# Two weight loads and two casts change places in GpSimd's opening queue

## Chip, core and metric

The kernel runs on one core of a Trainium2 chip. The metric is the device time of one execution in microseconds (us), the median of several runs. A core has five engines that work side by side and meet only at semaphores: TensorE (PE, matrix products; PEld is its loading of weights), VectorE (DVE), ScalarE (ACT), GpSimd (POOL) and SyncE (SP, which here only issues transfers). Transfers (DMAs) are issued by SP, ACT or GpSimd, each into a queue of its own, and are carried out by 16 DMA engines that all the queues share.

## What is computed

Attention over 8 batches, 8 heads, 576 positions and head size 64, followed by a gated feed-forward block over the 4608 token rows. Heads 0 to 3 see a window of the last 32 positions ("plain"), heads 4 to 7 every fourth position of the last 128 ("dilated"):

```python
mask_plain = (rel >= 0) & (rel < window)
mask_dil = (rel >= 0) & (rel < window * dilation) & (rel % dilation == 0)
attn = softmax(where(mask, scale * q @ k.T, -1e9))     # per batch and head
x = (attn @ v).transpose(0, 2, 1, 3).reshape(4608, 512)
out = (gelu(x @ w_gate) * (x @ w_val)) @ w_out         # 512 -> 1536 -> 512
```

Inputs and output are 32-bit floats in memory; the kernel computes in 16-bit floats.

## The kernel before

**Tiling.** Attention is cut into 32 units, four for each batch: a unit is a pair of heads. Units 0 and 1 of a batch are plain, 2 and 3 dilated. For a unit, PE makes scores (S), ACT takes the exponential (P), PE makes the denominators (D) and numerators (N), and DVE multiplies the numerator by the reciprocal (X), which writes 576 columns of one of the four `xT` tiles. The feed-forward part is cut into 8 chunks of 512 tokens. A chunk has a gate phase (line 597: 12 column blocks of 128, each with four products for the gate and four for the value, one per `xT` tile) and an output phase (line 604). The attention of batch c+1 is woven into the output phase of chunk c. The order of every engine is written out by hand, as strings of words in `gate_words` and `out_words`: "N1@00" is the numerators of unit 1, "X1" its multiplication, a bare number that many feed-forward products.

**The opening.** Batch 0 has to be computed before there is anything to weave it into. Its order on PE ends with

```python
"... N0@40 X0 D3@00 N2@60 X2 A3 N3@20 1 N1@00 X1 X3 G V 15 g0 u0 g1 u1 8 g2 u2 8 ..."
```

so N0, D3, N2, N3, one feed-forward product, N1, then 15 more products (with the one, column blocks 0 and 1), then block after block of 8. PE takes them strictly in this order.

**Block-diagonal v.** For units 0 and 1 of batch 0 the numerators use v in a block-diagonal form, the tile `vdiag`, 128 columns for each of 9 blocks of 64 positions. `load_v(0, 0, True)` (line 665) issues four loads on SP's queue, one for each half (64 partitions) of each unit, into the 32-bit tile `stage` (line 235). `cast_diag(g)` (lines 250 to 255) copies unit g out of `stage` into `vdiag` on GpSimd, in two casts of 64 partitions x 576 columns; each waits for its own load. N0 waits for the casts of unit 0, N1 for those of unit 1.

**Weights.** `w_gate` and `w_val` are loaded in four pieces of columns, `WC` (line 77): piece 0 holds column blocks 0 and 1, piece 1 blocks 2 and 3, piece 2 blocks 4 to 7, piece 3 blocks 8 to 11. `load_w(i)` (line 148) issues two loads, `wg` then `wv`, on GpSimd's queue; they turn 32-bit into 16-bit on the way. GpSimd has 8 semaphores for its loads and takes them in turn, so the issue of a load waits until the load eight places before it has landed.

**GpSimd's queue** is, in this order: masks; four loads of q and k of the dilated heads (line 176, into tails of `xT`); six loads of v (lines 295 and 303); `load_w(0, 1)`; the four casts of `vdiag`; `load_w(2)`; then, from `second()` (line 686), `load_w(3)`, two loads of q and k of batch 1 (line 690), two more (line 176), three of `w_out` (`wo`, line 156), six of v, and the masks of line 312 on.

**What hangs on it later.** `second()` also issues `load_v(1, 1, True)` on SP: the four loads of v for batch 1, which `gated` holds back until the first load of `w_out` has landed. GpSimd casts them at line 248, and N4, the first numerators of batch 1 (line 432), waits for that cast.

Of the kernel before, what the change touches and what calls it, by code (L numbers as in the profile page):

```python
# [21 lines left out]
def kernel(  # L22
# [125 lines left out]
    def load_w(*parts):  # L148

        for i in parts:  # L150
            for t, w in ((wg_t, moe_w_gate), (wv_t, moe_w_val)):
                src = w[:, WC[i][0] : WC[i][1]].rearrange("(kc p) n -> p kc n", p=P)
                nc.gpsimd.dma_start(out=t[i], in_=src)
# [43 lines left out]
    def st_of(i):  # L197
        return stage[:, 1280 * i : 1280 * i + 1280]
# [51 lines left out]
    def cast_diag(g):  # L250

        st = st_of(0)[:, 0:1152].rearrange("p (e d) -> p e d", d=D)
        at = slice(NB2 * g, NB2 * g + NB2)
        for x in range(2):
            nc.gpsimd.tensor_copy(diag[half_of(x), at, half_of(x)], st[half_of(x), at])  # L255

    def half_of(x, swap=0):
        y = x ^ (1 if swap else 0)
        return slice(64 * y, 64 * y + 64)
# [138 lines left out]
    def bias_first(n, bank):  # L398

        base = base_of(n, bank)  # L400
        tiles["bias", n] = True

        def part(c0, step, k, w, src=None, st=False):
            rhs = at2(bias, BQ if src else 0, [[0, k], [1, w]])
            o = at2(psf, base + c0, [[step, k], [1, w]])
            nc.tensor.matmul(o, ident, rhs, start=st, stop=False, skip_group_check=True)

        if is_plain(n):
            part(0, BQ, 5, BQ, st=True)
            part(5 * BQ, BQ, 3, BQ, st=True)  # L410
            part(8 * BQ, BK, 1, BK)
        else:
            part(0, 176, 3, BQ, st=True)
            part(BQ, 176, 2, 80)
            part(2 * 176 + BQ, 176, 2, 80, st=True)
            part(3 * 176, 176, 1, BQ)
            part(LD - BK, BK, 1, BK, src=True)
# [260 lines left out]
    biases()  # L678
    zero()
    bias_first(0, 4)  # L680
    load_w(0, 1)
    for g in range(2):
        cast_diag(g)
    load_w(2)

    def second():
# [170 lines left out]
```

## Time and profile before

| | us |
|---|---|
| median of 3 runs (328.08 to 329.41) | 328.7 |
| the profiled execution | 329.31 |
| its span, first to last instruction | 327.6 |
| PE busy in the span | 320.5 |
| GpSimd busy in the span | 78.6 |
| DMA engines, first third of the span | nearly always busy |

The span is what the profiler saw of one execution; the 1.71 us between it and that execution's own time lie around it. PE is busy 98% of the span, so a stall of PE shows nearly one for one in the time, and there is little else to gain or lose. All waits of PE fall into the first 53 us: after that no wait of PE is recorded. The first line of the slices of the profile shows how busy the DMA engines are over the span (40 slices of 8.19 us, in tenths):

```profile
DMA  8999996998897898989889657972000100020002
```

A row of the timeline below gives start, duration, engine, line, operation, output and input, the number of instructions merged, and in brackets the idle time ahead of it with what ended it. A row of the chain of waits gives start, duration and what the chain went through. Times in both count from the start of the span.

### The profile page before, as it was taken

How to read it: one execution, taken by the hardware profiler on the slowest of the kernel's cores; microseconds unless marked ns; L12 is line 12 of the kernel's file. 1: busy time of each engine (PE TensorE's matmuls, PEld its weight loads, DVE VectorE, ACT ScalarE, POOL GpSimd, SP SyncE). 2: the span in 40 equal slices, each digit the busy share in tenths (PEclk: the TensorE clock that was granted, in tenths of full speed). 3: DMA queues.
4: the chain of work that ended last, by engine and by line, in shares of the span. 5: the costliest groups of instructions: out<-in, count | busy, mean ns of one | idle time of the engine just before them, and what ended most of it. 6: DMA issues, size and time to landing. Idle time of an engine off the chain costs nothing.

```text
span 327.6 us, 7705 instructions
## 1 busy us (share of the span) xinstructions
PE 320.5 (98%) x3191; PEld 155.8 (48%) x3191; DVE 138.8 (42%) x208; ACT 169.5 (52%) x258; POOL 78.6 (24%) x126
## 2 busy tenths in 40 slices
PE   7899999999999999999999999999999999999995
PEld 4754544444544454445444454445444544444443
DVE  6763545434443444333633344334443354204410
ACT  2663566535863576347734783368436853234321
POOL 8783453402331340233224113311000000000000
PEclk9999999999999999999999999999999999999999
DMA  8999996998897898989889657972000100020002
GB/s 187 184 198 206 202 194 143 258 192 192 189 257 166 163 197 168 251 212 200 206 202 249 150 170 182 226 180 75 30 0 33 68 35 0 0 105 25 0 34 96
DMA packets 106659, 47.70 MB, mean 146 GB/s; under 512 B 83584, under 2 KB 102144, under 8 KB 106624
## 3 DMA queue, kind: packets, MB, share of 16 engines
q1 hardware_dynamic: 96352, 39.47, 52.4%
q0 software_dynamic: 9712, 7.08, 14.2%
q10 hardware_dynamic: 560, 0.66, 0.7%
q8 instruction: 25, 0.41, 0.5%
q14 instruction: 10, 0.08, 0.1%
HBM read 37.75 MB, written 9.44 MB: 144 GB/s over the span
## 4 chain that ended last, share of the span: by engine, by line
PE 83%; DMA 14%; SPq 1%; POOL 1%; issue 0%; DVE 0%; POOLq 0%
PE ps L597 51%; PE ps L604 26%; DMA stage<-in_v_dram 5%; PE ps L432 5%; DMA wo<-in_moe_w_out_dram 5%; DMA wg<-in_moe_w_gate_dram 2%; DMA u_all<-in_q_dram 2%; SPq L235 1%; PE ps L628 1%; POOL v L248 0%; POOL vdiag L255 0%; SPq L662 0%; DVE osb L637 0%; POOLq L248 0%
## 5 line engine op out<-in xcount | busy, mean ns | idle before, releaser
L759 DVE SCALAR_TENSOR_TENSOR u_all<-g,ps 128x512 f16<-128x512 f16 x108 | 74.2, 688 | 105.8 <-PE ps L597 92.2
L754 ACT ACTIVATE g<-ps 128x512 f16<-128x512 f32 x108 | 64.4, 597 | 104.4 <-PE ps L597 104.4
L597 PE MATMUL ps<-xT,wg 128*128 128x512 f16 x432 | 114.7, 379 | 0.2
L597 PE MATMUL ps<-xT,wv 128*128 128x512 f16 x432 | 114.0, 379 | 0.5 <-DMA wv<-in_moe_w_val_dram 0.5
L604 PE MATMUL ps<-wo,u_all 128*128 128x512 f16 x420 | 97.0, 380 | 0.0
L597 PEld LDWEIGHTS <-wv 128*128 128x128 f16 x432 | 42.1, 98 | 51.9 <-DMA wv<-in_moe_w_val_dram 1.2
L597 PEld LDWEIGHTS <-wg 128*128 128x128 f16 x432 | 42.1, 98 | 50.8 <-DMA wg<-in_moe_w_gate_dram 0.2
L604 PEld LDWEIGHTS <-u_all 128*128 128x128 f16 x420 | 38.7, 98 | 44.5 <-issue 0.3
L588 DVE TENSOR_TENSOR xT<-ps,rb 128x576 f16<-128x576 f32 x32 | 28.8, 938 | 27.1 <-PE ps L432 23.9
L462 ACT ACTIVATE P<-ps 128x832 f16<-128x832 f32 (+1 forms) x32 | 25.3, 834 | 14.4 <-PE ps L432 14.4
L248 POOL CAST v<-stage 128x1152 f16<-128x1152 f32 x13 | 15.0, 1154 | 67.5 <-DMA stage<-in_v_dram 67.5
L615 ACT ACTIVATE osb<-ps 128x512 f32<-128x512 f32 x31 | 18.5, 598 | 21.3 <-PE ps L604 20.9
L211 POOL CAST s<-stage 128x640 f16<-128x640 f32 x24 | 17.0, 735 | 39.0 <-DMA stage<-in_q_dram 23.7
L559 ACT ACTIVATE lg<-ps 128x576 f32<-128x576 f32 x30 | 18.2, 650 | 4.2 <-issue 2.2
L565 ACT ACTIVATE rb<-lg 128x576 f32<-128x576 f32 x30 | 19.0, 688 | 0.1
L223 POOL CAST s<-stage 128x512 f16<-128x512 f32 x24 | 14.4, 628 | 10.3 <-DMA stage<-in_q_dram 8.5
L467 DVE TENSOR_TENSOR P<-P,two_p 128x832 f16<-128x832 f16 x14 | 9.3, 670 | 13.4 <-ACT P L462 13.3
L467 DVE TENSOR_TENSOR P<-P,two_d 128x768 f16<-128x768 f16 x14 | 8.2, 592 | 13.2 <-ACT P L462 12.4
L779 ACT ACT_TABLE_LOAD x9 | 11.5, 1283 | 0.2
L432 PEld LDWEIGHTS <-q 64*64 64x64 f16 x576 | 7.7, 107 | 6.7 <-issue 5.5
L432 PEld LDWEIGHTS <-v 64*64 64x64 f16 x600 | 7.4, 107 | 5.9 <-issue 4.2
L432 PE MATMUL ps<-q 64*64 64x96 f16 (+2 forms) x576 | 9.9, 203 | 0.3 <-DVE q L334 0.3
(66 smaller groups left out, 123.0 us busy)
## 6 DMA issues: line engine op xcount, KB each, us to landing
out_dram<-osb SPq DMA_DIRECT2D x35, 256.0 KB, 3.2
stage<-in_v_dram SPq DMA_DIRECT2D x32, 144.0 KB, 3.5
stage<-in_q_dram SPq DMA_DIRECT2D x24, 128.0 KB, 3.5
stage<-in_k_dram SPq DMA_DIRECT2D x24, 128.0 KB, 2.9
stage<-in_q_dram SPq DMA_DIRECT2D x6, 512.0 KB, 4.8
stage<-in_k_dram SPq DMA_DIRECT2D x6, 512.0 KB, 5.6
stage<-in_v_dram SPq DMA_DIRECT2D x24, 128.0 KB, 3.0
wo<-in_moe_w_out_dram POOLq DMA_DIRECT2D x3, 512.0 KB, 15.9
```

The costliest lines, as they stand in the source:

```text
L211: nc.gpsimd.tensor_copy(s16[:, 1280 * t + 640 * g : 1280 * t + 640 * g + 640].rearrange("p (k c) -> p k c", k=5), st_of(i).rearrange("p (k ...
L432: nc.tensor.matmul(o[cols], lhs[rows], rhs[rows], start=st, stop=end, skip_group_check=True)
L462: nc.scalar.activation(pt[:, 0 : src.shape[1]], src, AF.Exp, bias=0.0, scale=scale)
L467: nc.vector.tensor_tensor(pt, pt, mask, ALU.mult)
L559: nc.scalar.activation(lg, psf[:, c0 : c0 + S], AF.Ln)
L565: nc.scalar.activation(rb, tiles.pop(("lg", n)), AF.Exp, scale=-1.0)
L588: nc.vector.tensor_tensor(dst, num, rb, ALU.mult)
L597: nc.tensor.matmul(ps[:, bank, :], w[:, kc, ns], xT[kc][:, tok], start=first, stop=end)
L604: nc.tensor.matmul(ps[:, bank, :], u_all[:, fc, tb * P : (tb + 1) * P], wo_t[fc // 4][:, fc % 4, :], start=(fc == 0), stop=(fc == NNB - 1),)
L615: nc.scalar.activation(osb, ps[:, bank, :], AF.Copy, bias=0.0, scale=1.0 / USCALE)
L754: nc.scalar.activation(g, ps[:, gate_banks(c, args[0])[0], :], AF.Gelu)
L759: nc.vector.scalar_tensor_tensor(u_all[:, nb, :], tiles.pop(("g", nb)), USCALE, val, ALU.mult, ALU.mult)
```

## The change

`load_w(0, 1)` is split: the casts of unit 0 go between weight piece 0 and piece 1, and those of unit 1 behind piece 1. Nothing else changes; the other engines keep their order, and the functions are as printed above.

```diff
     zero()
     bias_first(0, 4)
-    load_w(0, 1)
-    for g in range(2):
-        cast_diag(g)
+    load_w(0)
+    cast_diag(0)
+    load_w(1)
+    cast_diag(1)
     load_w(2)
```

In GpSimd's queue this gives: `wg` and `wv` of piece 0, two casts (unit 0), `wg` and `wv` of piece 1, two casts (unit 1), `wg` and `wv` of piece 2. The number of instructions is the same.

## The prediction

> **What bounds the kernel now.** I read the share of each engine first:
>
> ```profile
> PE 320.5 (98%) x3191; PEld 155.8 (48%) x3191; DVE 138.8 (42%) x208; ACT 169.5 (52%) x258; POOL 78.6 (24%) x126
> ```
>
> PE is the bound; a change on GpSimd counts only where it makes PE wait or stop waiting. So next the waits of PE (total, times, longest), up to 40 us and then from 27 to 60 us:
>
> ```profile
> PE ps L597 <- DMA wv<-in_moe_w_val_dram: 0.5, 1, 0.5
> PE ps L421 <- POOL vdiag L255: 0.4, 1, 0.4
> ...
> PE ps L432 <- POOL v L248: 0.3, 1, 0.3
> ```
>
> The same view from 56 us to the end is empty: whatever PE has lost by N4 (the third line) is lost for good, and nothing later takes it up. What holds N4 stands in the chain of waits of the first 60 us:
>
> ```profile
> 17.62 6.88 DMA wg<-in_moe_w_gate_dram
> ...
> 24.79 15.08 DMA wo<-in_moe_w_out_dram
> ...
> 41.90 9.43 DMA stage<-in_v_dram
> ...
> 51.48 1.16 POOL v L248
> ...
> 52.67 0.58 PE ps L432 x40
> ```
>
> From 17.62 to 52.67 us the chain runs through transfers, not through PE. N4 starts when the v of batch 1 has landed and is cast, and that v stands behind all the weights. The third place to look is GpSimd's timeline, where the change is made:
>
> ```profile
> 10.94 0.77 POOL L153 DMA_DIRECT2D wg<-in_moe_w_gate_dram  x1 [0.75 <-DMA xT<-in_q_dram]
> 11.70 0.76 POOL L153 DMA_DIRECT2D wv<-in_moe_w_val_dram  x1
> 12.96 0.74 POOL L153 DMA_DIRECT2D wg<-in_moe_w_gate_dram  x1 [0.51 <-DMA v<-in_v_dram]
> 13.69 0.75 POOL L153 DMA_DIRECT2D wv<-in_moe_w_val_dram  x1
> 14.42 0.68 POOL L255 CAST vdiag<-stage 64x576 f16<-64x576 f32 x1
> 15.43 1.38 POOL L255 CAST vdiag<-stage 64x576 f16<-64x576 f32 x2 [0.32 <-DMA stage<-in_v_dram]
> 17.01 0.67 POOL L255 CAST vdiag<-stage 64x576 f16<-64x576 f32 x1 [0.19 <-DMA stage<-in_v_dram]
> 17.62 0.74 POOL L153 DMA_DIRECT2D wg<-in_moe_w_gate_dram  x1
> ```
>
> The second cast of unit 0 starts at 15.43 because its v lands then, not because GpSimd comes late. Last, the DMA view from the start to 17 and to 18 us: q0 is GpSimd's queue, with packets, MB and share.
>
> ```profile
> q0 software_dynamic: 2655, 1.37, 60.5%
> ...
> q0 software_dynamic: 3028, 1.55, 64.8%
> ```
>
> The loads ahead of the weights are four of 144 KB, four of 64 and two of 16, 0.885 MB; with the two 256 KB pieces of `load_w(0)` 1.409 MB. That amount is passed between 17 and 18 us, at 17.2: there the engines begin piece 1. The trace's landing marks, sixteen for each load, agree: `wv` of piece 0 marks at 17.2 to 17.7 on 14 DMA engines, at 19.0 and 19.3 on two that lag; piece 1's `wg` at 18.5 to 19.0, the laggards at 19.8 and 20.6. Spacing is 1.3 us per 256 KB, 2.5 per 512 KB, with no gap.
>
> **What the Trainium skill says.** "DMA: Bandwidth & Descriptors", section "Queues, rings and completion order": each DMA engine works off its own ring of a queue in order and alternates between queues. The evenly spaced marks agree. The same page, "Why a DMA increments its semaphore by 16 and not by 1": a load has landed only when all its engines have marked, so the slowest decides; PE's wait for `wg` of piece 0 indeed ended at 18.00, with the last mark (17.95), not with the first fifteen (16.0 to 16.4). Its "Latency and other measured facts" gives about 1 us from a GpSimd load to its first byte. The trace does not agree: the first such load is issued at 3.16 and the 6.0 to 6.2 us window is the first that shows a packet of q0, 3.0 us after the issue begins. And "TensorE: Matmul & The Clock Gate", Part 1, says PE slows after about 3.4 us of idleness; the waits below are shorter, and the granted clock is 1.00 in every 2 us window of the first 56 us.
>
> **The change part by part.** GpSimd: both loads of piece 0 as before, to 12.46. The first cast of unit 0 waits for its v (last mark 14.21), some 14.3 to 15.0; the second runs from 15.43 as before. A cast frees the queue after 0.61 us (17.01 to 17.62), so `wg` of piece 1 is issued at 16.04 instead of 12.96, 3.08 later, and `wv` at 16.04 + 0.74 = 16.78. Then unit 1's casts: 17.52 and 18.13, done by 18.80 instead of 17.68. Piece 2 follows at 18.74 instead of 17.62 (+1.12), piece 3 at about 20.2, the four loads after it end near 24.4. The first `wo` load waits for `wg` of piece 2 (24.50) anyway, so its issue at 24.79 need not move: the 1.53 us it idles now cover the 1.12.
>
> N0 gains nothing: its second cast is held by the landing at 15.3. The 0.41 us wait stays.
>
> N1 loses. It starts at 18.23 now; its cast will end at 18.80, so about 18.87, 0.64 later, and behind it PE's whole queue. But four steps on PE stops for piece 2's `wv` from 26.53 to 27.07 (0.55 us). If that still lands at 27.0, PE stands at 27.15 instead of 27.07: 0.64 - 0.55 = about 0.1 us. X1 moves with N1, and X3, ending near 21.3, is just in time for its products, due at 21.8.
>
> Piece 1 itself is due on PE at 22.05 + 0.64 = 22.7 (`wg`) and 23.55 (`wv`). Issue to first packet is the price the trace shows only once, at the start (3.0 us, when other transfers filled the engines too). From below: the page's 1 us behind the end of the issue, 16.78 + 1.0 = 17.8. From above: the shown 3.0 us, 16.04 + 3.0 = 19.04. I take the shown one, since q0 took most of the traffic as soon as it appeared, so it was not queued behind the others. Fourteen engines finish piece 0 at about 17.35 to 17.5 and have nothing else to do (q1, SP's queue, moves no packet from 16 to 40 us). They idle 19.04 - 17.45 = 1.6 us (0.4 from below). The two laggards run dry only at 19.0 to 19.3 and hardly idle. So `wg` lands at about 20.6 either way, set by them: on time. `wv` and pieces 2 and 3 follow without a second gap (piece 2's first packet is ready by 18.74 + 3.0 = 21.7, the engines come to it at about 21.7), their landings still near 24.5, 27.0, 29.5 and 32.2. Up to there the late issue is hidden behind the two slow engines.
>
> But the fourteen now run 1.5 us behind their old schedule, and the lead they had is gone. In before it is used up at the last of the k loads of batch 1: its marks have their middle at 37.0 and their end at 37.3, and `wo` marks ten of sixteen within 39.5 to 39.9. From there all sixteen decide. So `wo` lands about 1.4 us late, SP lets the v of batch 1 go 1.4 late, these end 1.4 late, then the cast, then N4. PE's own 0.1 is covered by that wait, and nothing later makes up for it. The lost time is the idle time of the engines, 1.6, less what the two undelayed engines save on average (1.6 x 14/16 = 1.4). Against the profiled run: 329.31 + 1.4 = 330.7. That run lies 0.6 above the median of the runs, so against the median 328.7 + 1.4 = 330.1.
>
> **Rivals.** B, the gap is hidden: the first packet comes at 17.8 or earlier, or the later loads end on engines that never ran dry. For it: the two laggards set every landing of the weights. Against: by 39.9 us ten marks bunch. Then 0.1 us is left from N1 and even this may vanish at N4: 328.7 + 0.1 = 328.8.
>
> C, slower: all sixteen engines run dry, the laggards too. The place is the ring between the pieces; it decides once the first packet comes later than 19.3, that is from 3.3 us behind the issue on. From then on every 0.1 us costs 0.1. At 3.8 us the gap is 19.84 - 17.45 = 2.4, less a few tenths for the laggards: +2.2, 330.9. For it: the one price shown is one sample, and `stage` loads may land later than before, which pushes the issue too. Against: it needs 0.3 us more than shown.
>
> D, faster: with piece 1 out of the way, the v of unit 0 lands earlier than 15.30, N0 starts up to 0.41 earlier, and N4 gains its 0.30. Against: piece 1 stood behind piece 0 in the ring and moved nothing before 17.2. Price at best -0.4: 328.3.
>
> That the change doesn't do what it says is excluded: the order of the instructions shows the casts moved.
>
> **Numbers.** A 0.52, B 0.20, C 0.23, D 0.05. About 0.5% (1.6 us) is what a measurement can tell from no change. A with its bounds, 0.9 to 1.7, and runs that scatter by a few tenths gives 0.18 slower, 0.34 same; B 0.20 same; C 0.22 slower, 0.01 same; D 0.04 faster, 0.01 same. Together faster 0.04, same 0.56, slower 0.40. The range reaches from B less its scatter, 328.5, to C, 331.2; A's own is 329.6 to 330.5.
>
> **What would show it.** Right: `wg` of piece 1 issued near 16.0; q0 nearly still between 17.5 and 19; N0 at 16.15 and N1 near 18.9; `wo` landing near 41.3; PE's wait at N4 near 1.6 instead of 0.3, and none behind it. Wrong: q0 moving without a gap (B), a longer wait of PE for piece 1 or 2 (C), or N0 before 16 (D).

## The result and the profile after

The change makes the kernel slower: 330.01 us median (328.81 to 331.17) against 328.78 us (328.08 to 329.41), 14 runs each, ratio 1.0037 with a 95% interval of 1.0025 to 1.0048. That is +1.2 us. The profiled execution took 330.15 us with a span of 328.4; the one of before 329.31 with 327.6.

The timeline of GpSimd after the change, in the same columns as before:

```profile
12.86 0.74 POOL L153 DMA_DIRECT2D wv<-in_moe_w_val_dram  x1 [1.54 <-DMA xT<-in_k_dram]
13.72 0.66 POOL L255 CAST vdiag<-stage 64x576 f16<-64x576 f32 x1
14.98 0.66 POOL L255 CAST vdiag<-stage 64x576 f16<-64x576 f32 x1 [0.61 <-DMA stage<-in_v_dram]
15.59 0.74 POOL L153 DMA_DIRECT2D wg<-in_moe_w_gate_dram  x1
16.32 0.75 POOL L153 DMA_DIRECT2D wv<-in_moe_w_val_dram  x1
17.11 1.39 POOL L255 CAST vdiag<-stage 64x576 f16<-64x576 f32 x2
18.44 0.74 POOL L153 DMA_DIRECT2D wg<-in_moe_w_gate_dram  x1
```

GpSimd now stands still for 0.61 us until the second half of unit 0's v has landed, and piece 1 of the weights stands behind that wait: its `wg` is issued at 15.59 instead of 12.96. Piece 2 follows at 18.44 instead of 17.62.

What this does to the DMA engines shows in the DMA view cut into windows of 1 us. The lines are those of q0, GpSimd's queue, with packets, MB and share; first the kernel before, from 17 to 18 and from 20 to 21 us:

```profile
q0 software_dynamic: 373, 0.19, 138.1%
...
q0 software_dynamic: 209, 0.19, 120.9%
```

and after, in 17 to 18, 18 to 19, 20 to 21 and 21 to 22 us:

```profile
q0 software_dynamic: 189, 0.09, 87.0%
...
q0 software_dynamic: 392, 0.20, 144.4%
...
q0 software_dynamic: 187, 0.11, 93.6%
...
q0 software_dynamic: 200, 0.20, 123.7%
```

The steady flow of 0.19 MB a microsecond breaks twice, ahead of piece 1 and ahead of piece 2. Together 0.10 + 0.08 MB are not moved, which is 0.9 us of flow. Two more profiles below have their loads in this order. They show the first break as large (0.10 and 0.07 MB are moved from 17 to 18 us) and the second one smaller (0.16 and 0.17 MB from 20 to 21 us), so the second varies from one execution to the next. The chain of waits of the first 60 us shows where the lost flow goes:

```profile
18.44 5.95 DMA wg<-in_moe_w_gate_dram
...
24.68 16.57 DMA wo<-in_moe_w_out_dram
...
43.28 8.70 DMA stage<-in_v_dram
...
52.13 1.16 POOL v L248
...
53.33 0.58 PE ps L432 x40
```

From `wg` of piece 2 on it is the same chain as before. The first `wo` load ends at 24.68 + 16.57 = 41.25 instead of 39.87, the v of batch 1 at 51.98 instead of 51.33, and N4 starts at 53.33 instead of 52.67. The waits of PE from 27 to 60 us are one line:

```profile
PE ps L432 <- POOL v L248: 1.1, 1, 1.1
```

It stood at 0.3. From 60 us on PE records no wait. From the start of N4 to the end of the span is 275.1 us after and 274.9 before: nearly the whole loss lies ahead of N4.

### The profile page after: what moved, and what is told of

Same layout as the page of the kernel before. It is cut to its first block, busy times and chain, and to the rows that moved or that the text cites. A ratio compares the mean times of both kernels' runs of the same rounds, so it can differ in the third digit from the quotient of the medians.

```text
span 328.4 us, 7705 instructions
## 1 busy us (share of the span) xinstructions
PE 320.2 (97%) x3191; PEld 155.7 (47%) x3191; DVE 141.1 (43%) x208; ACT 169.6 (52%) x258; POOL 79.2 (24%) x126
## 4 chain that ended last, share of the span: by engine, by line
PE 83%; DMA 13%; POOL 1%; SPq 1%; issue 0%; DVE 0%; POOLq 0%
PE ps L597 51%; PE ps L604 26%; PE ps L432 5%; DMA wo<-in_moe_w_out_dram 5%; DMA stage<-in_v_dram 5%; DMA wg<-in_moe_w_gate_dram 2%; DMA u_all<-in_q_dram 2%; PE ps L628 1%; SPq L235 1%; POOL vdiag L255 1%; POOL v L248 0%; POOL wv L153 0%; POOL wg L153 0%; SPq L662 0%; DVE osb L637 0%
## 5 line engine op out<-in xcount | busy, mean ns | idle before, releaser
L467 DVE TENSOR_TENSOR P<-P,two_p 128x832 f16<-128x832 f16 x14 | 10.5, 755 | 12.8 <-ACT P L462 12.7
L467 DVE TENSOR_TENSOR P<-P,two_d 128x768 f16<-128x768 f16 x14 | 9.3, 676 | 12.5 <-ACT P L462 10.2
```

The costliest lines, as they stand in the source:

```text
L467: nc.vector.tensor_tensor(pt, pt, mask, ALU.mult)
```

## The experiments

Theory A is that of the prediction: the late issue lets the DMA engines run dry between the pieces, all later transfers slide, and PE pays at N4. Its first rival, N, is simpler: the casts of unit 1 come later, N1 stands on PE's path, and PE pays there. All times are given against the kernel before on the same chip; one ratio step of 0.001 is 0.33 us.

**N1 late, no load late.**

```diff
     load_w(0, 1)
-    for g in range(2):
-        cast_diag(g)
+    cast_diag(0)
     load_w(2)
+    cast_diag(1)
```

> Order: piece 0, piece 1, casts of unit 0, piece 2, casts of unit 1. N1 comes as late as in the change (its casts end near 18.8 us), but no load is issued later than in the kernel before. Theory A (the time is lost because DMA engines run dry between the pieces): no dry stretch, wo lands near 39.9 us, the wait of PE at N4 stays near 0.3 us, time as before within 0.4 us. Rival N (the late casts of unit 1 on PE's path cost the time): as slow as the change, +1.2 us.

Measured 0.9997 (0.9988 to 1.0006): no change. Its timeline of PE has N1 as late as the change has it (18.55), with a wait for the cast, and N4 without one:

```profile
18.64 0.55 PE L421 MATMUL ps<-P,vdiag 128*128 128x96 f16 x10 [0.45 <-POOL vdiag L255]
...
52.01 0.56 PE L432 MATMUL ps<-P,v 64*64 64x96 f16 x40
```

So an N1 as late as that of the change costs nothing that can be measured here. Piece 2 was issued earlier than in the kernel before (15.67 against 17.62), which could have made up for something. The profile of the change itself shows more: at `wv` of piece 2, where PE waited before, it is no later than before (first line before, second line the change):

```profile
27.07 1.04 PE L597 MATMUL ps<-xT,wv 128*128 128x512 f16 x4 [0.55 <-DMA wv<-in_moe_w_val_dram]
...
26.98 1.04 PE L597 MATMUL ps<-xT,wv 128*128 128x512 f16 x4
```

N1 was 0.32 us late (18.55 against 18.23), and the wait that was there anyway has taken that up. Rival N falls for the change. An N1 that is 2 us late is another matter, as a run below shows.

**N1 on time, piece 1 later still.**

```diff
     load_w(0)
     cast_diag(0)
-    load_w(1)
     cast_diag(1)
+    load_w(1)
     load_w(2)
```

(The diff is against the change.)

> Order: piece 0, casts of unit 0, casts of unit 1, piece 1, piece 2. N1 is on time, but piece 1 is issued near 17.6 us, 1.5 to 2 us later than in the change. Theory A: dry stretch of about 2.7 us ahead of piece 1 and none ahead of piece 2; wo lands 2 to 2.7 us later than before, a longer wait at N4, +2.0 to +2.6 us. Rival N: time as before, since N1 is on time.

Measured 1.0112 (1.0091 to 1.0133), +3.7 us: the direction of A, but more than it allowed. Piece 1 was issued at 17.33. The DMA view in 17 to 18, 18 to 19 and 19 to 20 us:

```profile
q0 software_dynamic: 41, 0.02, 15.9%
...
q0 software_dynamic: 31, 0.02, 29.1%
...
q0 software_dynamic: 254, 0.13, 106.8%
```

The queue all but stops for two microseconds, and it stays at or below 0.16 MB a microsecond until 24 us, although all four loads of pieces 1 and 2 were issued back to back from 17.33 to 20.3. PE now waits three times:

```profile
PE ps L597 <- DMA wv<-in_moe_w_val_dram: 1.6, 1, 1.6
...
PE ps L432 <- POOL v L248: 1.3, 1, 1.3
PE ps L597 <- DMA wg<-in_moe_w_gate_dram: 1.1, 1, 1.1
```

The weights themselves come too late now. N4 starts at 55.99; from there to the end (331.0) is again 275.0 us.

**The two dry stretches apart.** The first kernel was to have only piece 1 late, the second only piece 2. `load_w` is altered so that `wg` and `wv` of a piece can be issued apart; in its notation 20 is `wg` and 21 `wv` of piece 2, 10 and 11 those of piece 1. The diffs here and in the next pair give the new order alone, on one line.

```diff
+    load_w(0); cast_diag(0); load_w(1, 20); cast_diag(1); load_w(21)     # first stretch only
```

```diff
+    load_w(0, 10); cast_diag(0); load_w(11); cast_diag(1); load_w(2)     # second stretch only
```

> Order: piece 0, casts of unit 0, piece 1, wg of piece 2, casts of unit 1, wv of piece 2. Piece 1 is issued as late as in the change (near 15.6 us), wg of piece 2 as early as before (near 17). Theory A: only the dry stretch ahead of piece 1 is left, about 0.8 of the 1.4 us; +0.5 to +0.9 us. If the second stretch is what costs: as before.

> Order: piece 0, wg of piece 1, casts of unit 0, wv of piece 1, casts of unit 1, piece 2. wg of piece 1 is issued as before, so no dry stretch ahead of it; piece 2 comes near 18 us, 0.4 later than before. Theory A: at most 0.5 us dry ahead of piece 2, +0.1 to +0.5 us. If the second stretch is what costs: as slow as the change.

The second measured 1.0017 (1.0006 to 1.0028), +0.6 us, just above what was expected. But its profile has `wg` of piece 2 issued at 17.46, no later than in the kernel before (17.62); what came later was `wv` of piece 1 (15.05 against 13.69). So this run does not show what a late piece 2 costs. The first missed: 1.0039 (1.0028 to 1.0049), +1.3 us, all of the loss. Its DMA view, in 17 to 18, 20 to 21 and 21 to 22 us, says why the edit did not do what it was to do:

```profile
q0 software_dynamic: 210, 0.11, 108.0%
...
q0 software_dynamic: 176, 0.12, 96.2%
...
q0 software_dynamic: 177, 0.18, 111.4%
```

The second dry stretch is there all the same, though `wg` of piece 2 was issued at 16.68, earlier than in the kernel before.

**Is it the cast behind that load?** Two more orders: `wg` of piece 2 between the two casts of unit 1, and both loads of piece 2 ahead of them.

```diff
+    load_w(0); cast_diag(0); load_w(1); cast_diag(1, (0,)); load_w(20); cast_diag(1, (1,)); load_w(21)
```

```diff
+    load_w(0); cast_diag(0); load_w(1, 2); cast_diag(1)
```

> As the change, but wg of piece 2 is issued between the two casts of unit 1 (near 17.5 us instead of 18.44). Theory A with about 2.2 us from issue to packets: the first dry stretch stays, the second nearly goes; +0.5 to +1.0 us, wo near 40.7 us. If the first stretch alone brings the whole loss: +1.2 us as the change and as the run with wg of piece 2 ahead of both casts.

> Order: piece 0, casts of unit 0, pieces 1 and 2, casts of unit 1. One dry stretch of about 0.8 us ahead of piece 1, and none ahead of piece 2, since both loads of piece 2 are issued by 17.5 us; N1 about 1.3 us later than in the change. If a cast behind the issue of wg of piece 2 is what slowed that load in the earlier run, its marks come evenly here. Theory A: +0.6 to +1.0 us, of which the late N1 is up to 0.8 at N4.

Measured 1.0043 (1.0027 to 1.0059) and 1.0048 (1.003 to 1.0067). Neither regained anything. The second has nothing between the loads of pieces 1 and 2 (issued from 15.93 to 18.9), and still its DMA view runs, in 19 to 20, 20 to 21 and 21 to 22 us:

```profile
q0 software_dynamic: 310, 0.15, 120.5%
...
q0 software_dynamic: 254, 0.13, 122.7%
...
q0 software_dynamic: 150, 0.12, 90.1%
```

In this run the casts of unit 1 follow right behind the loads, from 18.93 on. In the run with both casts ahead of piece 1 no cast follows, and there too the flow stays low from 20 to 24 us, with `wg` of piece 2 issued at 18.79. So neither a cast behind the loads nor a late issue of piece 2 is needed for the later stretch; no run leaves out both. What these orders share is the first one: once the queue has run dry, the loads behind come in with gaps even when they were issued 3 to 4 us before.

The time of the second run has another cause, though, at least in its profile. N1 waits for its cast and starts 2.14 us later than in the kernel before:

```profile
20.37 0.83 PE L421 MATMUL ps<-P,vdiag 128*128 128x96 f16 x10 [1.75 <-POOL vdiag L255]
21.02 1.47 PE L597 MATMUL ps<-xT,wg 128*128 128x512 f16 x3
```

The granted clock of PE is then 0.50 from 21 to 23 us, and the products for column block 2 start at 25.66 instead of 22.05, 3.61 us late. PE waits for nothing behind N1, neither for weights nor at N4. So the late N1 and the lowered clock bring the loss there, and the lost flow is hidden behind them. That execution took 331.93 us, against a median of 330.31. The four longest of the ten executions (330.87 to 331.93) are the four with a mean clock of 0.995, the others had 0.998 to 1.000. How much the lost flow counts in those others was not seen.

In the profile of the first run PE takes up the late N1 in a wait for `wv` of piece 2 (1.3 us) and starts on it at 28.53 instead of 27.07. There is no wait at N4, so the weights bring the whole loss.

**Where the loss reaches PE.** In `out_words(0)` three of the ten output products behind N4 and N5 are put ahead of them, in the change and in the kernel before (a part of one line):

```diff
-D6@52+D7@22 N4@50+N5@20 X4 l7 X5 l6 r6 r7 10 N6
+D6@52+D7@22 3 N4@50+N5@20 X4 l7 X5 l6 r6 r7 7 N6
```

> The change, and three of the ten output products that stand behind N4 and N5 on PE stand ahead of them (0.65 us). Theory A, with N4 as the place where the loss becomes time: the products fill 0.65 us of the wait at N4, 0.4 to 0.7 us faster than the change, +0.5 to +0.8 against before. If the loss comes in elsewhere on PE: as slow as the change.

> The kernel before with the same three products ahead of N4. Theory A: its wait at N4 is 0.3 us at most, so 0 to 0.3 us faster than before, and the distance to the change so altered is about 0.6 us instead of 1.2. If the loss comes in elsewhere on PE: that distance stays 1.2.

Measured 1.0015 (1.0005 to 1.0025) for the change so altered and 0.9996 (0.9988 to 1.0004) for the kernel before. Work of 0.65 us put into the wait at N4 gives back about 0.7 us of the change's 1.2 (by the intervals, 0.2 to 1.2), and nothing measurable in the kernel before. So N4 is where much of the loss becomes time, most of it by the middle of that range. The wait at N4 is gone from both profiles. In that of the altered change another line has come up instead, so some of the loss can also be taken by the weights:

```profile
PE ps L597 <- DMA wv<-in_moe_w_val_dram: 0.9, 1, 0.9
```

**Releasing the v of batch 1 earlier.** It was let go by the last q and k load of batch 1 (the last load that `load_eights(1)` issues, which it now returns) instead of by the first `wo` load:

```diff
-        gate["dma"] = wo[0]
+        gate["dma"] = eights
```

> The change, and the v of batch 1 is released by the last load of q and k of batch 1 (lands near 38.7 us) instead of by the first load of w_out (41.25). Theory A: that v lands earlier, the wait at N4 falls from 1.05 us towards 0 to 0.5, 0.5 to 1 us faster than the change. Rival N: nothing gained at N4 matters, 330.0 us as the change.

> The kernel before with the same earlier release of the v of batch 1 (37.3 instead of 39.9 us). Theory A: the wait of 0.3 us at N4 vanishes, 0 to 0.4 us faster than before, and the distance to the change with the same release is under 0.7 us instead of 1.2. Rival N: that distance stays 1.2 us.

Both missed: 1.0034 (1.0021 to 1.0047) for the change, 1.0003 (0.9994 to 1.0013) for the kernel before. The distance is 1.0 us (1.0034 against 1.0003), not to be told from the 1.2 it had. In the change that v was released near 39 instead of 41.3 us and landed at 51.65 instead of 51.98. So a release 2.3 us earlier brings the landing forward by 0.3 us: what this v waits for is mostly the engines, not its release. q1 moves 0.06 MB from 40 to 45 us in the kernel before, while q0 is at work on `wo` and moves 0.92 MB.

**A version to beat both.** The first order of this section with the three products ahead of N4.

> The order with the casts of unit 1 behind piece 2, and three output products ahead of N4. Theory A: no load is issued later than before and the wait at N4 is covered; 0 to 0.4 us faster than before. Rival N: +1 us.

Measured 0.9999 (0.9991 to 1.0008): nothing gained. No order tried beats the kernel before.

**All orders side by side.** q0 moved 1.35 MB from 17 to 24 us in the kernel before, 0.193 a microsecond. What an order moves less in that window, divided by 0.193, is the flow it lost:

| order | MB, 17 to 24 us | flow lost, us | time (95% interval), us |
|---|---|---|---|
| casts of unit 1 last | 1.40 | -0.3 | -0.1 (-0.4 to 0.2) |
| `wv` of piece 1 behind the casts of unit 0 | 1.31 | 0.2 | 0.6 (0.2 to 0.9) |
| `wg` of piece 2 between the casts | 1.20 | 0.8 | 1.4 (0.9 to 1.9) |
| the change | 1.19 | 0.8 | 1.2 (0.8 to 1.6) |
| piece 1 late, `wg` of piece 2 ahead of the casts of unit 1 | 1.11 | 1.2 | 1.3 (0.9 to 1.6) |
| pieces 1 and 2, then unit 1 | 1.06 | 1.5 | 1.6 (1.0 to 2.2) |
| both casts ahead of piece 1 | 0.73 | 3.2 | 3.7 (3.0 to 4.4) |

The MB come from one profiled execution each. The two altered kernels with the loads in the order of before gave 1.29 and 1.36, the two with those of the change 1.18 and 1.24, so a step of 0.3 us means little. At its ends the table is clear: with no flow lost no time is lost, and 3.2 us of lost flow go with 3.7 us. The orders between 0.8 and 1.5 can't be told apart by their times, and the row "pieces 1 and 2, then unit 1" is no evidence for the flow, since its profile has the time lost at N1.

## Why the prediction was right, and where its terms were off

330.1 was forecast and 330.01 measured; the mechanism was the forecast one, a dry stretch ahead of piece 1 that PE pays at N4. That the numbers are so close is in part luck. By its steps:

**GpSimd's queue.** `wg` of piece 1 was put at 16.04 and came at 15.59, because unit 0's v landed 0.45 earlier in this execution. N0 starts at 16.13 (16.15 before): no gain, as said. N1 was put at 18.87 and came at 18.55, and the wait for `wv` of piece 2 took it up as said: those products start at 26.98 against 27.07 before. The run with the casts of unit 1 last, in which N1 is late and no load is, agrees that this step costs nothing.

**The first dry stretch was mis-sized.** The step "At 16.04 + 3.0 = 19.04 ... they idle 1.6 us" took 3.0 us from issue to packets. The flow came back near 17.7, 2.1 us behind the issue at 15.59: 17 to 18 us is short of 0.10 MB, or 0.5 us. The single sample at the start of the kernel was too long for the price, and the lower bound from the Trainium skill ("DMA: Bandwidth & Descriptors", "Latency and other measured facts": 1 us, here behind the end of the issue at 16.33, so 17.3) somewhat too short.

**The second dry stretch was left out.** "`wv` and pieces 2 and 3 follow without a second gap" is wrong: 20 to 21 us is short of 0.08 MB, 0.4 us. The two steps hang together. The prediction had the engines come to piece 2 at about 21.7, just when its packets would be ready; since the flow came back early, they were through with piece 1 at about 20.4 and had to wait. With both stretches, some 0.8 to 0.9 us of flow are lost instead of 1.4.

**The path to PE held in part.** The landings of the weights stayed near their old times behind the slow engines, as said: the last mark of `wg` of piece 2 at 24.40 (24.50 before), of its `wv` at 26.93 (27.03), while the mean of their sixteen marks is 0.76 and 0.72 later. `wo` was to land 1.4 late and landed 1.38 late (41.25), but this agreement is luck: the mean of its sixteen marks is only 0.71 later, and the last engine ended 0.62 behind the fifteenth (0.19 in before). (The prediction counted ten marks of `wo` from 39.5 to 39.9 in before; there are nine.) The next link, a v of batch 1 that is late because its release is late, is weak, as the runs with the earlier release show. The mean of its marks is 0.65 later, and so is the last one, not 1.4; the wait at N4 is 1.05, not 1.6. So the engines run some 0.7 us late from piece 2 to the v of batch 1, half of what was forecast. In the two profiles the time differs by 0.84 us, in the medians by 1.23, because the profiled execution of before is itself 0.53 above its median and that of the change 0.14. So the forecast time owes its closeness to errors that partly cancel, a first stretch that was too long and a second one that was missing, and to medians that lie further apart than the two profiles.

**The rivals.** B (the gap hidden) fell: the flow breaks. C (slower by running all sixteen engines dry) is what the run with both casts ahead of piece 1 shows, at an issue 1.7 us later than that of the change; the change stays short of it. D fell: N0 gained nothing.

**Open:** why loads that were issued early come in with gaps once the queue has been dry. Neither a late issue nor a cast behind the loads is needed for it, though no run leaves out both. The place may tell something: the later stretch lies in or next to the time at which q0 has moved 1.93 MB, the end of piece 1 (20.4 us in the change, 21.2 with pieces 1 and 2 ahead of unit 1). How long a load takes to be made ready behind another was not measured by itself.

## What to carry to other kernels

A queue of loads has a lead, the time by which issue runs ahead of the engines, and an instruction that waits for a transfer spends it for all loads behind. Before moving such an instruction forward, work out from the cumulated bytes when the engines will finish what is already queued; here the next issue had to come some 2 to 2.5 us before that, and once the queue had run dry even 3 to 4 us did not keep the flow whole. Look for the price far downstream: here GpSimd's order at 16 us was paid by PE at 53 us, while the operation moved forward gained nothing, since its own input was what it waited for. And read from each profile where PE waits, before a lost flow is called the cause: two orders that lose much the same time can lose it at different places.

## What the hardware showed unexpectedly

From a load's issue on GpSimd to the return of full flow took 2.1 us (15.59 to about 17.7) and some 2.5 us (18.44 to about 21) in the change, against 3.0 us to the first packet at the start of the kernel. After a dry stretch the flow needed several microseconds to be even again: with both casts ahead of piece 1 it was still at 0.15 MB a microsecond or less from 21 to 24 us, with all loads of two pieces issued by 20.3 us. At `wv` of piece 0 the last of the sixteen engines ended 1.6 to 2.1 us behind the middle one in all thirteen profiles, and it alone sets the landing; that lead of the others is what kept the late piece 1 of the change from stopping PE at once. At `wg` of piece 2 the last engine is 1.55 us behind the middle of the marks before and 0.66 in the change: much of the lead has been used up.

A wait of PE of 1.75 us was followed by a granted clock of 0.50 for 3.4 us (20.5 to 23.9 us, in the profile of the order with pieces 1 and 2 ahead of the casts of unit 1), though the prediction took about 3.4 us of idleness to be needed for that. It does not always follow: waits of 1.1 and 1.6 us, with both casts ahead of piece 1, left the clock at 1.00.
